# One fixed order for three engines, carried on through block 0's first layer

## The chip, the cores and the metric

The kernel runs on one core of a Trainium2 chip. A core has a matrix engine (TensorE, PE in the rows), VectorE (DVE), ScalarE (ACT), GpSimd (POOL) and a queue engine (SyncE, SP) that issues the transfers. The metric is the device time of one execution in microseconds, as the median of several runs.

## The reference

Eight heads of attention over chunks of 64 tokens make x of 4608 x 512; two layers with hidden widths of 2048 and 1024 follow.

```python
scores = (q_c @ k_c.T) / 8                       # per head, chunks of 64 tokens
attn = exp(scores - max); attn /= sum(attn) + 1e-9
x = attn @ v_c                                   # then as [4608, 512]
h = x @ w_in; y = (h * sigmoid(h)) @ w_out       # 512 -> 2048 -> 512
h = y @ w_in2                                    # 512 -> 1024
solu = h * softmax(h)
out = (layernorm(solu) * g_ln) @ w_out2          # 1024 -> 512
```

## The kernel before, in words

The tokens are worked in 9 blocks of 512, each of four tiles of 128 (block 0 has tiles 0 to 3, block 1 tiles 4 to 7, which come in the order 4, 6, 5, 7). Every fp32 operand is split into a high and a low fp16 half, and a product takes three matmuls (high by high, high by low, low by high). Blocks 0 and 1 multiply plainly; from block 2 on a form with seven products of half blocks is used.

The weights come as 64-bit words, 48 items of 512 KB: 16 of the first layer, 16 of the second, then those of the last two. SP fetches an item (`fetch`, L929, tile `wst`, four buffers, so that item i is fetched when item i - 4 has been decoded). Then it is decoded: `d1` scales on ACT (L133, into a bank of PSUM), `d2` joins bits in three DVE instructions (L140, L141, L143), and `d3` splits, the high half on ACT (L114), the low one on POOL (L118). `weights(n)` does n times d3, d1, d2.

In block 0's first layer PE works 16 groups of 12 matmuls (`h_group`, L418 to L420). Each is followed by a Silu on ACT (L422) and by `g_split`: the high half of the gate on ACT, the low half on DVE (L119). PSUM's eight banks go round in the order of the program, so a group or a d1 can need the bank whose gate low was eight allocations earlier.

Behind the groups come eight steps (`step(s)`, each followed by half of one of the four output tiles of the second layer: `x_part`, 24 matmuls, L716 to L718). The steps hold block 1's attention: q, k and v of a tile are halved (`prep_qk`, `prep_v`: ACT high, POOL low, v's low on DVE), then scores (`a_scores`: L232 to L234 on PE, the maximum L236 and the subtraction L245 on DVE, the exponential on ACT), the division (`a_norm`), a transposing transfer issued by SP (L260), and the product with v (`a_pv`, L277 to L279). `AT_S` says in which steps the scores of tiles 4, 6, 5 and 7 stand; the products stand in steps 3, 4, 6 and 7.

What sets the order: a scheduler orders the instructions by the order of the program and by priorities. The list `START` overrides it for ACT, DVE and PE up to the end of block 0's attention: each of its steps is held behind the last instruction that earlier steps put on each engine (`queue`). In the kernel before, the list ends ahead of the first layer. There the table `NW0` says how many items are decoded behind each group, and block 1's halvings of q, k and v are held behind the last step of the list alone.

Of the kernel before, what the change touches and what calls it, by code (L numbers as in the profile page):

```python
# [11 lines left out]
AF = mybir.ActivationFunctionType  # L12
# [11 lines left out]
TPB = BLK // P  # L24
NB = NT // BLK
KD = DM // P
K1 = F1 // P
# [9 lines left out]
S_X = 2.0 ** 10  # L37
# [9 lines left out]
def fused(ctx: ExitStack, tc: tile.TileContext, qkv, w1, w2, w3, w4, g_ln, out):  # L47
# [6 lines left out]
    GH = A  # L54
    FIRST = 'qqqwqvwvwvvw'
    START = ('s0 m0 s1 m1 e0 s2 s3 e1 n0 m2 m3 d1 t0 e2 p0 n1 e3 a2 n2 t1 x0 t2 n3 p1 d1 d2 x1 d3 l0 t3 l1 p2 x2 d2 '
             'd1 l2 p3 x3 d3 l3 d2 d1 d3 d2 d1 d3 d2 d1')
    AT_S = (0, 1, 3, 4)
    NW0 = [2, 0, 0, 0, 3, 0, 2, 0, 1, 0, 3, 0, 1, 0, 3, 0]
    NX = [2, 3, 2, 1, 0, 6, 0, 2]  # L60
    NW1 = [2, 1, 2, 1, 1, 1, 1, 1, 1, 1, 1, 1, 1, 1, 1, 0]
    NX1 = [1, 0, 0, 1, 0, 1, 1, 0]
# [128 lines left out]

    def prep_qk(t, eng_l=G, ahead=True):
        with ExitStack() as behind_all:
            if t // TPB == 1:
                for i in queue.values():
                    behind_all.enter_context(tc.issue_after(i))
            qk_halves(t, eng_l, ahead)

# [10 lines left out]

    def prep_v(t):  # L210
        with ExitStack() as behind_all:
            if t // TPB == 1:
                for i in queue.values():
                    behind_all.enter_context(tc.issue_after(i))
            v_halves(t)

# [184 lines left out]
            split(y[:, 0], y[:, 1], t[i].rearrange("p t k n -> p (t k) n"), 1.0, A, V)  # L401


    gt, graw = {}, {}

    def g_of(b, f):
        if (b, f) not in gt:
# [5 lines left out]
    def h_group(b, f):  # L413
        xh, xl = xt[b][:, 0], xt[b][:, 1]
        wh, wl = w1t[f][:, 0], w1t[f][:, 1]
        ps = ps1.tile([P, BLK], F32, tag="mm", name="h_ps")
        for k in range(KD):
            T.matmul(ps, wh[:, k], xh[:, k], start=k == 0, stop=False)  # L418
            T.matmul(ps, wh[:, k], xl[:, k], start=False, stop=False)
            T.matmul(ps, wl[:, k], xh[:, k], start=False, stop=k == KD - 1)  # L420
        g = one.tile([P, BLK], F32, tag=f"h{f % 2}", name="g") if b else ps
        A.activation(g, ps, AF.Silu, scale=1.0 / (S_X * S_W))  # L422
        graw[f] = g

    def g_split(b, f, eng_h=V):
        return split(*g_of(b, f), graw.pop(f), S_G, eng_h, V)

# [537 lines left out]
    def weights(n=1):  # L967
        for _ in range(n):
            d3()
            d1()  # L970
            d2()
# [12 lines left out]
    nc.sync.dma_start(out=gs, in_=g_ln)  # L984


    parts = dict(s=f_scores, m=f_max, e=f_exp, a=f_sum, n=f_norm, t=f_turn, p=f_pv, x=f_high, l=f_low)
    steps = {"d1": d1, "d2": d2, "d3": d3, "w": weights}
    queue = {}
    for x in START.split():  # L990
        with ExitStack() as behind_all:
            for i in queue.values():
                behind_all.enter_context(tc.issue_after(i))
            done = steps[x]() if x in steps else parts[x[0]](int(x[1]))
        for i in done:
            queue[i.engine] = i

    load_v(TPB)
    second = [one.tile([P, NS, P], F16, tag=f"xb{i}", name="qb") for i in range(2)]
# [4 lines left out]
    for b in range(NB):  # L1004
        m = b * TPB + TPB
        more = b + 1 < NB
        if FAST <= b:
            q_alloc(b)
        for f in range(K1):
            if b < FAST:  # L1010
                if b == 1 and f in MHF:
                    n = MHF.index(f)
                    run(m_h(b - 1, MO[n], "m1", ("m2", ("h4", "h5"), ("h6", "h7"), ("h2", "h3"))[n]))
                if b == 1 and f in MOF:
                    run(m_out(b - 1, MO[MOF.index(f)]))
                h_group(b, f)
                if b == 0:
                    weights(NW0[f])
                    if f:
                        g_split(b, f - 1, GH)  # L1020
                else:
                    y = g_split(b, f, A)
                    with tc.high_priority(offset=-50):
                        weights(NW1[f])
                    with tc.high_priority(offset=1):
                        for p in range(8):
                            if W1F[p] == f:
                                w1_sums(p)
                    if f == QF:
                        load_qk(m, ("q8",))  # L1030
                        prep_qk(m, ahead=False)
            elif f % 8 == 0:
                if f and more:
                    load_qk(m, ("w1_14", "w1_15"))
                    prep_qk(m, ahead=False)
                if b == FAST:
                    for n in range(2):
                        run(m_h(b - 1, MO[f // 4 + n], *(("m1", "m2"), ("w2_5", "w2_4"))[n % 2]))
                if f and b == FAST:
                    for n in range(2):  # L1040
                        run(m_out(b - 1, MO[n]))
                elif b > FAST:
                    run(m_fast(b - 1, 1) if f else begun, in_turn(*(m_out(b - 1, MO[n]) for n in range(2) if f)))
                run(h_fast(b, f // 4), h_fast(b, f // 4 + 1))
        if b == 0:
            g_split(b, K1 - 1, GH)
        else:
            run(m_out(b - 1, MO[TPB - 2], low=more))
        if b == FAST - 1:
            ring.load()  # L1050
        def step(s):

            if not more:
                return
            if s == 0:
                if b < FAST - 1:
                    load_qk(m)
                    prep_qk(m)
                else:
                    load_qk(after(m))  # L1060
                prep_v(m)
            if b and s == 1:
                run(m_out(b - 1, MO[TPB - 1]))
            for i in VL.get(s, ()) if b >= FAST else ():
                load_v(m + ORDER[i] if i < TPB else after(m + ORDER[-1]))
            AT_P = (3, 4, 6, 7) if b == 0 else (3, 4, 5, 6)
            if s in AT_S:
                i = AT_S.index(s)
                n = m + ORDER[i]
                a_scores(n)  # L1070
                if i < 3:
                    prep_qk(m + ORDER[i + 1], V if b == 1 else G)
                a_norm(n, eng_l=V if b else G)
            if s in AT_P:
                i = AT_P.index(s)
                a_pv(m + ORDER[i])
            if b == 0:
                with tc.high_priority(offset=-50):
                    weights(NX[s])
            if b == FAST and s in W3S:  # L1080
                w3_sums(W3S.index(s))
            if b == 1:
                weights(NX1[s])
            for n in range(4):
                if b == 1 and W2F[n] == s:
                    w2_sums(n // 2, n % 2)

        if b < FAST:
            for s in range(8):
                step(s)  # L1090
                x_part(b, s // 2, s % 2)
        else:
            begun = m_fast(b, 0, alt=not more)
            x_fast(b, step, begun)
# [54 lines left out]
```

## Time and profile before

| | |
|---|---|
| median of 3 runs | 1174.11 us (1173.61 to 1174.71) |
| the profiled execution's own time | 1173.64 us |
| its span | 1171.9 us |
| busy over the span | PE 1123.9 (96 %), DVE 917.4 (78 %), ACT 803.3 (69 %), POOL 250.4 (21 %) |
| PE's mean granted clock | 0.993 |

The profile is of one execution; times count from the start of its span, and 1.7 us of the execution lie outside it. PE's share is an average over all 9 blocks. The change lies in the first 130 us, where the weights are decoded beside the work.

### The profile page before, as it was taken

To read this page: it belongs to the slowest core of one execution; us is meant where nothing else is said; L and a number is where in the kernel's file an instruction comes from. 1 tells how busy PE (TensorE), PEld (TensorE's weight loads), DVE (VectorE), ACT (ScalarE), POOL (GpSimd) and SP (SyncE) were. 2 spreads that over 40 slices of the span, in tenths; PEclk is the share of its full clock that TensorE was granted. 3 is DMA by queue.
4 is the path that set the end of the run, shared out by engine and by line. 5 is a ranking of instruction groups with operands and counts; after the bars stand their busy time and mean duration, and the time that the engine had idled before them with its cause. 6 is when DMAs were issued, how large, how long until landed. Compare 5 with 4: busy or idle time off the path is not lost.

```text
span 1171.9 us, 23546 instructions
## 1 busy us (share of the span) xinstructions
PE 1123.9 (96%) x9036; PEld 767.0 (65%) x9036; DVE 917.4 (78%) x1639; ACT 803.3 (69%) x1460; POOL 250.4 (21%) x243
## 2 busy tenths in 40 slices
PE   7899898998999999999999999999999999999998
PEld 5344343444657865887678767876787777777853
DVE  6898998587678788889778987898689868886453
ACT  6986678675667777856775687568756875587253
POOL 3655323344101510021003100310021002100001
PEclk8999999999999999999999999999999999999999
DMA  7657488543537654786568557856776667565604
GB/s 280 217 186 209 150 234 270 166 140 113 140 113 222 180 157 132 200 228 179 150 189 235 175 157 192 230 169 160 179 235 173 162 177 223 168 163 145 207 19 117
DMA packets 205169, 209.18 MB, mean 178 GB/s; under 512 B 120192, under 2 KB 130432, under 8 KB 205056
## 3 DMA queue, kind: packets, MB, share of 16 engines
q1 hardware_dynamic: 205056, 207.68, 61.8%
q8 instruction: 70, 1.15, 0.4%
q14 instruction: 43, 0.35, 0.1%
HBM read 156.24 MB, written 24.12 MB: 154 GB/s over the span
## 4 chain that ended last, share of the span: by engine, by line
PE 64%; DVE 13%; ACT 9%; issue 6%; DMA 5%; POOL 2%; ACTq 0%; SPq 0%; POOLq 0%; DVEq 0%
PE o_ps L894 5%; PE o_ps L887 5%; PE o_ps L886 5%; PE pa L655 4%; PE pa L654 4%; PE pa L656 4%; PE pa L547 3%; PE pa L549 3%; PE pa L548 3%; PE pa L781 2%; PE pa L779 2%; PE pa L780 2%; DVE vbl L119 2%; PE pb L549 2%; PE pb L547 2%
## 5 line engine op out<-in xcount | busy, mean ns | idle before, releaser
L114 ACT ACTIVATE q<-hc 128x512 f16<-128x512 f32 x196 | 120.5, 627 | 42.8 <-DVE hc L634 15.6
L119 DVE SCALAR_TENSOR_TENSOR q<-hc,q 128x512 f16<-128x512 f32 x196 | 137.9, 719 | 10.9 <-ACT q L114 8.7
L118 POOL TENSOR_TENSOR qbl<-qk,qbh 64x512 f16<-64x512 f32 x54 | 71.2, 1319 | 264.7 <-ACT qbh L114 220.3
L654 PE MATMUL pa<-q,ring 128*128 128x256 f16 x448 | 122.1, 273 | 0.0
L656 PE MATMUL pa<-q,ring 128*128 128x256 f16 x448 | 122.1, 273 | 0.0
L655 PE MATMUL pa<-q,ring 128*128 128x256 f16 x448 | 122.1, 273 | 0.0
L886 PE MATMUL o_ps<-w4h,uT 128*128 128x512 f16 x288 | 109.1, 379 | 0.3 <-DVE e L837 0.3
L887 PE MATMUL o_ps<-w4l,uT 128*128 128x512 f16 x288 | 109.2, 379 | 0.0
L850 POOL TENSOR_TENSOR c<-c,mhalf 128x2 f32<-128x2 f32 (+1 forms) x22 | 14.1, 639 | 387.3 <-DVE c L849 385.1
L548 PEld LDWEIGHTS <-ring 128*128 128x128 f16 x784 | 77.0, 98 | 16.7 <-issue 6.1
L547 PEld LDWEIGHTS <-ring 128*128 128x128 f16 x784 | 77.0, 98 | 11.3 <-DMA ring<-w1s 0.7
L655 PEld LDWEIGHTS <-ring 128*128 128x128 f16 x784 | 76.7, 98 | 11.1
L654 PEld LDWEIGHTS <-ring 128*128 128x128 f16 x784 | 76.7, 98 | 11.1
L549 PEld LDWEIGHTS <-ring 128*128 128x128 f16 x784 | 77.0, 98 | 9.2
L656 PEld LDWEIGHTS <-ring 128*128 128x128 f16 x784 | 76.7, 98 | 8.8
L894 PE MATMUL o_ps<-w4h,uT 128*128 128x512 f16 x288 | 70.2, 379 | 0.0
L547 PE MATMUL pa<-xb,ring 128*128 128x256 f16 x224 | 61.0, 273 | 3.5 <-DVE hc L605 3.1
L547 PE MATMUL pa<-x,ring 128*128 128x256 f16 x224 | 61.0, 273 | 2.0 <-ACT hc L565 2.0
L549 PE MATMUL pa<-x,ring 128*128 128x256 f16 x224 | 61.2, 273 | 0.0
L549 PE MATMUL pb<-x,ring 128*128 128x256 f16 x224 | 61.1, 273 | 0.0
L548 PE MATMUL pb<-x,ring 128*128 128x256 f16 x224 | 61.1, 273 | 0.0
L654 PE MATMUL pb<-q,ring 128*128 128x256 f16 x224 | 61.1, 273 | 0.0
(282 smaller groups left out, 3483.7 us busy)
## 6 DMA issues: line engine op xcount, KB each, us to landing
ring<-w1s SPq DMA_DIRECT2D x196, 256.0 KB, 3.3
ring<-w2s SPq DMA_DIRECT2D x196, 256.0 KB, 3.7
wst<-w SPq DMA_DIRECT2D x48, 512.0 KB, 4.2
qk<-qkv SPq DMA_DIRECT2D x29, 512.0 KB, 3.9
vs<-qkv SPq DMA_DIRECT2D x36, 256.0 KB, 2.9
out<-o SPq DMA_DIRECT2D x36, 256.0 KB, 2.3
w1s<-ws SPq DMA_DIRECT2D x32, 128.0 KB, 2.0
w2s<-ws SPq DMA_DIRECT2D x16, 256.0 KB, 2.0
```

Source lines behind the costliest of these rows:

```text
L114: ready[0] = A.activation(dst_h, src, AF.Copy, scale=scale).ins
L118: return G.tensor_tensor(out=dst_l, in0=src, in1=dst_h, op=ALU.subtract).ins
L119: return V.scalar_tensor_tensor(out=dst_l, in0=src, scalar=scale, in1=dst_h, op0=ALU.mult, op1=ALU.subtract).ins
L547: T.matmul(ps[:, c], wh, x[:, 0, k], start=first, stop=False, skip_group_check=True)
L548: T.matmul(ps[:, c], wh, x[:, 1, k], start=False, stop=False, skip_group_check=True)
L549: T.matmul(ps[:, c], wl, x[:, 0, k], start=False, stop=k == 1, skip_group_check=True)
L654: T.matmul(ps[:, c], wh, g[:, 0], start=first, stop=False, skip_group_check=True)
L655: T.matmul(ps[:, c], wh, g[:, 1], start=False, stop=False, skip_group_check=True)
L656: T.matmul(ps[:, c], wl, g[:, 0], start=False, stop=q == 1 and f == 3, skip_group_check=True)
L886: T.matmul(ps, uh[:, k], w4h[:, k, :], start=k == 0, stop=False)
L887: T.matmul(ps, uh[:, k], w4l[:, k, :], start=False, stop=False)
L894: T.matmul(ps, ul[:, k], w4h[:, k, :], start=False, stop=k == K2 - 1)
```

## The change

The list goes on. `START` loses its last four steps, the loop over it becomes the function `in_order`, and block 0's first layer calls it for each group f with `d1 d3 d2 h{f} g{f}`: decode, group and gate are now held behind one another on each engine, where the scheduler placed them before. Behind the layer come two more d1 and one set of weights, outside the list. Of block 1's halvings only those of tile 4 are held, q and k behind gate 14's split and v behind gate 15's; the other tiles' halvings are free. In block 0 the scores of tiles 4 and 6 stand one step later each, those of the last two where they were.

```diff
     START = (...
-             'd1 l2 p3 x3 d3 l3 d2 d1 d3 d2 d1 d3 d2 d1')
+             'd1 l2 p3 x3 d3 l3 d2 d1 d3 d2')
-    NW0 = [2, 0, 0, 0, 3, 0, 2, 0, 1, 0, 3, 0, 1, 0, 3, 0]
...
     def prep_qk(t, eng_l=G, ahead=True):
         with ExitStack() as behind_all:
-            if t // TPB == 1:
-                for i in queue.values():
+            if t == TPB:
+                for i in gates[14]:
                     behind_all.enter_context(tc.issue_after(i))
...
     def prep_v(t):
         with ExitStack() as behind_all:
-            if t // TPB == 1:
-                for i in queue.values():
+            if t == TPB:
+                for i in gates[15]:
                     behind_all.enter_context(tc.issue_after(i))
...
     def g_split(b, f, eng_h=V):
-        return split(*g_of(b, f), graw.pop(f), S_G, eng_h, V)
+        low = split(*g_of(b, f), graw.pop(f), S_G, eng_h, V)
+        if b == 0:
+            gates.append((ready[0], low))
+        return low
...
+    def in_order(xs):
+        for x in xs.split():
+            with ExitStack() as behind_all:
+                for i in queue.values():
+                    behind_all.enter_context(tc.issue_after(i))
+                done = steps[x]() if x in steps else parts[x[0]](int(x[1:]))
+            for i in done:
+                queue[i.engine] = i
+
+    in_order(START)
...
-                h_group(b, f)
                 if b == 0:
-                    weights(NW0[f])
-                    if f:
-                        g_split(b, f - 1, GH)
+                    in_order(f"d1 d3 d2 h{f} g{f}" if f else "h0 g0")
                 else:
+                    h_group(b, f)
                     y = g_split(b, f, A)
...
         if b == 0:
-            g_split(b, K1 - 1, GH)
+            d1()
+            weights()
+            d1()
...
-            if s in AT_S:
-                i = AT_S.index(s)
+            at_s = AT_S if b else (1, 2, 3, 4)
+            if s in at_s:
+                i = at_s.index(s)
```

How the rows move. On DVE, in the middle of the first layer, before (`g<-h_ps,g` is a gate's low half, `wp` and `wy` are a decode's tiles):

```order
L119 SCALAR_TENSOR_TENSOR g<-h_ps,g 128x512
L143 SCALAR_TENSOR_TENSOR wy<-wst,wp 128x512
L119 SCALAR_TENSOR_TENSOR g<-h_ps,g 128x512
L140 TENSOR_SCALAR wp<-wp 128x512 x2
L141 SCALAR_TENSOR_TENSOR wp<-wst,wp 128x512 x2
L143 SCALAR_TENSOR_TENSOR wy<-wst,wp 128x512 x2
```

and in the changed kernel, where every slot reads like this one:

```order
L118 SCALAR_TENSOR_TENSOR g<-h_ps,g 128x512
L139 TENSOR_SCALAR wp<-wp 128x512
L140 SCALAR_TENSOR_TENSOR wp<-wst,wp 128x512
L142 SCALAR_TENSOR_TENSOR wy<-wst,wp 128x512
L118 SCALAR_TENSOR_TENSOR g<-h_ps,g 128x512
```

Before, decodes of two items and gates are mixed; now each slot is one decode of three instructions in a row and one gate.

On ACT at the end of the layer, before (`wp<-wst` is d1, `w2t<-wy` is d3, `h_ps<-h_ps` the Silu, `qbh` and `kb` belong to tile 4):

```order
L133 ACTIVATE wp<-wst 128x512 x2
L114 ACTIVATE g<-h_ps 128x512
L422 ACTIVATE h_ps<-h_ps 128x512
L114 ACTIVATE w2t<-wy 128x512
L114 ACTIVATE g<-h_ps 128x512
L133 ACTIVATE wp<-wst 128x512
L422 ACTIVATE h_ps<-h_ps 128x512
L114 ACTIVATE w2t<-wy 128x512
L114 ACTIVATE g<-h_ps 128x512
L114 ACTIVATE qbh<-qk 64x8x64
L133 ACTIVATE wp<-wst 128x512
L114 ACTIVATE qbh<-qk 64x8x64
```

and in the changed kernel, up to tile 4's k:

```order
L132 ACTIVATE wp<-wst 128x512
L113 ACTIVATE w2t<-wy 128x512
L132 ACTIVATE wp<-wst 128x512 x2
L113 ACTIVATE qbh<-qk 64x8x64
L132 ACTIVATE wp<-wst 128x512
L421 ACTIVATE h_ps<-h_ps 128x512
L113 ACTIVATE w2t<-wy 128x512
L113 ACTIVATE g<-h_ps 128x512
L113 ACTIVATE qbh<-qk 64x8x64
L113 ACTIVATE kb<-qk 128x512
L113 ACTIVATE vbh<-vs 64x8x64 x2
```

Three d1 (items 19 to 21, the first two in one row) and half of tile 4's q now stand ahead of the last Silu, the rest of tile 4's q and its k behind the last gate.

On DVE around tile 4's first reduce (`am<-s_ps`, L236 before, L235 now), before:

```order
L119 SCALAR_TENSOR_TENSOR g<-h_ps,g 128x512
L143 SCALAR_TENSOR_TENSOR wy<-wst,wp 128x512
L119 SCALAR_TENSOR_TENSOR g<-h_ps,g 128x512
L140 TENSOR_SCALAR wp<-wp 128x512
L236 TENSOR_REDUCE am<-s_ps 128x8
L141 SCALAR_TENSOR_TENSOR wp<-wst,wp 128x512
L119 SCALAR_TENSOR_TENSOR g<-h_ps,g 128x512
L245 TENSOR_TENSOR ae<-s_ps,am 128x512
```

and in the changed kernel:

```order
L118 SCALAR_TENSOR_TENSOR g<-h_ps,g 128x512
L142 SCALAR_TENSOR_TENSOR wy<-wst,wp 128x512
L140 SCALAR_TENSOR_TENSOR wp<-wst,wp 128x512
L118 SCALAR_TENSOR_TENSOR vbl<-vs,vbh 64x8x64 x2
L142 SCALAR_TENSOR_TENSOR wy<-wst,wp 128x512
L139 TENSOR_SCALAR wp<-wp 128x512 x2
L140 SCALAR_TENSOR_TENSOR wp<-wst,wp 128x512 x2
L142 SCALAR_TENSOR_TENSOR wy<-wst,wp 128x512 x2
L139 TENSOR_SCALAR wp<-wp 128x512
L140 SCALAR_TENSOR_TENSOR wp<-wst,wp 128x512
L142 SCALAR_TENSOR_TENSOR wy<-wst,wp 128x512
L139 TENSOR_SCALAR wp<-wp 128x512
```

Before, the reduce stands ahead of the last gate's low half; now it stands behind it, behind v's two lows and behind four more decodes (24 instead of 20). On PE one thing moves: before, the scores of tile 4 stand ahead of the second layer's first half and those of tile 6 ahead of its second; now each stands one half later. On SP the load of tile 5's q and k, which stood among the first loads, now stands behind the fetch of item 23, since its buffer is freed by tile 4's k.

## Rows read from the trace of the kernel before

**Rows 1.** Windows: each engine's busy us (x instructions), PE's clock, DMA share, GB/s.
```profile
core 0: us, PE busy (x) PEld busy (x) DVE busy (x) ACT busy (x) POOL busy (x), PEclk, DMA share, GB/s
24.00:70.00 46.00, 42.10 (x205) 18.96 (x205) 40.57 (x67) 38.30 (x69) 25.87 (x23) 1.00 0.63 211
70.00:100.00 30.00, 25.00 (x185) 12.63 (x181) 27.55 (x48) 23.96 (x54) 21.65 (x19) 0.94 0.66 191
100.00:130.00 30.00, 25.34 (x198) 12.62 (x196) 27.02 (x44) 18.69 (x45) 11.40 (x9) 1.00 0.61 188
130.00:195.00 65.00, 57.66 (x281) 27.34 (x280) 61.66 (x111) 51.58 (x90) 23.66 (x23) 1.00 0.75 221
```

**Rows 2.** Timeline of PE, 37 to 131 us: start, us, instruction [idle before <-releaser].
```profile
37.76 0.38 PE L418 MATMUL h_ps<-x,w 128*128 128x512 f16 x1 [0.63 <-DVE g L119]
...
46.30 0.38 PE L418 MATMUL h_ps<-x,w 128*128 128x512 f16 x1 [3.20 <-DVE g L119]
...
73.38 0.38 PE L716 MATMUL x_ps<-g,w2t 128*128 128x512 f16 x1 [2.91 <-DVE g L119]
...
92.58 0.20 PE L277 MATMUL x_ps<-pT,vbh 128*128 128x64 f16 x1 [2.10 <-DMA pT<-ae]
...
128.57 0.38 PE L418 MATMUL h_ps<-x,w 128*128 128x512 f16 x1 [1.26 <-ACT x L114]
```

**Rows 3.** Timeline of DVE, one decode and the next one's start.
```profile
23.93 0.69 DVE L140 TENSOR_SCALAR wp<-wp 128x512 int32<-128x512 int32 x1
24.66 0.69 DVE L141 SCALAR_TENSOR_TENSOR wp<-wst,wp 128x512 int32<-128x512 int32 x1
25.39 0.69 DVE L143 SCALAR_TENSOR_TENSOR wy<-wst,wp 128x512 int32<-128x512 int32 x1
25.99 0.69 DVE L140 TENSOR_SCALAR wp<-wp 128x512 int32<-128x512 int32 x1
```

**Rows 4.** Timeline of DVE around tile 4's first reduce.
```profile
74.15 0.69 DVE L119 SCALAR_TENSOR_TENSOR g<-h_ps,g 128x512 f16<-128x512 f32 x1 [0.23 <-ACT g L114]
74.75 0.69 DVE L140 TENSOR_SCALAR wp<-wp 128x512 int32<-128x512 int32 x1
75.35 0.68 DVE L236 TENSOR_REDUCE am<-s_ps 128x8 f32<-128x512 f32 x1
```

**Rows 5.** Timeline of ACT at the end of block 0's first layer.
```profile
71.47 0.62 ACT L133 ACTIVATE wp<-wst 128x512 f32<-128x512 f32 x1 [1.53 <-DMA wst<-w]
...
74.58 0.55 ACT L422 ACTIVATE h_ps<-h_ps 128x512 f32<-128x512 f32 x1
...
77.22 0.63 ACT L114 ACTIVATE qbh<-qk 64x512 f16<-64x512 f32 x1
...
77.87 0.63 ACT L114 ACTIVATE kb<-qk 128x512 f16<-128x512 f32 x1
...
78.52 1.28 ACT L246 ACT_TABLE_LOAD   x1
```

**Rows 6.** The tile wst on SP's queue, issues of 0:130 and of 66:71.
```profile
DMA to landing us min/median/max: 3.2/4.6/9.9
...
DMA to landing us min/median/max: 4.6/4.7/4.9
```

**Rows 7.** Timeline of POOL, lows of tile 4 and of its numerators.
```profile
76.87 2.38 POOL L118 TENSOR_TENSOR qbl<-qk,qbh 64x512 f16<-64x512 f32 x2
...
86.58 1.15 POOL L258 TENSOR_TENSOR ae<-ae 128x512 f16<-128x512 f32 x1
```

**Rows 8.** Timeline of PE, 155 to 200 us (block 1).
```profile
161.19 0.38 PE L418 MATMUL h_ps<-x,w 128*128 128x512 f16 x1 [1.66 <-ACT g L422]
...
179.33 0.27 PE L447 MATMUL wq<-w,ident 128*128 128x256 f16 x1 [2.86 <-DVE e L837]
```

**Rows 9.** Windows of 2 us each, columns as in rows 1.
```profile
74.00:76.00 2.00, 2.00 (x11) 0.91 (x10) 1.85 (x4) 2.00 (x5) 1.12 (x2) 1.00 0.59 190
...
94.00:96.00 2.00, 2.00 (x6) 0.76 (x5) 1.53 (x4) 1.18 (x2) 1.79 (x3) 0.50 0.74 197
...
96.00:98.00 2.00, 2.00 (x11) 0.83 (x9) 1.90 (x4) 1.19 (x3) 1.64 (x2) 0.95 0.97 278
```

More of the change, by code (lines that the diff above doesn't have):

```diff
@@ L401, in x_sums @@
             split(y[:, 0], y[:, 1], t[i].rearrange("p t k n -> p (t k) n"), 1.0, A, V)
-    gt, graw = {}, {}
+    gt, graw, gates = {}, {}, []
     def g_of(b, f):
@@ L419, in h_group @@
             T.matmul(ps, wh[:, k], xl[:, k], start=False, stop=False)
-            T.matmul(ps, wl[:, k], xh[:, k], start=False, stop=k == KD - 1)
+            i = T.matmul(ps, wl[:, k], xh[:, k], start=False, stop=k == KD - 1).ins
         g = one.tile([P, BLK], F32, tag=f"h{f % 2}", name="g") if b else ps
-        A.activation(g, ps, AF.Silu, scale=1.0 / (S_X * S_W))
+        j = A.activation(g, ps, AF.Silu, scale=1.0 / (S_X * S_W)).ins
         graw[f] = g
+        return [i, j]
     def g_split(b, f, eng_h=V):
-        return split(*g_of(b, f), graw.pop(f), S_G, eng_h, V)
+        low = split(*g_of(b, f), graw.pop(f), S_G, eng_h, V)
+        if b == 0:
+            gates.append((ready[0], low))
+        return low
     def flat(a, keep):
@@ L984, in fused @@
     nc.sync.dma_start(out=gs, in_=g_ln)
-    parts = dict(s=f_scores, m=f_max, e=f_exp, a=f_sum, n=f_norm, t=f_turn, p=f_pv, x=f_high, l=f_low)
+    parts = dict(s=f_scores, m=f_max, e=f_exp, a=f_sum, n=f_norm, t=f_turn, p=f_pv, x=f_high, l=f_low,
+                 h=lambda f: h_group(0, f), g=lambda f: [g_split(0, f, GH), ready[0]])
     steps = {"d1": d1, "d2": d2, "d3": d3, "w": weights}
     queue = {}
[L990 to L996, printed above, removed]
+    def in_order(xs):
[7 more added lines that the diff above has]
+    in_order(START)
     load_v(TPB)
```

## The prediction

> **What bounds the kernel now.** I read the windows by stage first, then TensorE's (PE's) waits in order of time, then the rows of the engines it waits for. The stages show two engines close to full: from 24 to 195 us VectorE (DVE) is busy 88 to 95 % of each stretch, and PE 83 to 92 % [rows 1]. The reader is to see that DVE leaves 10.9 us unused between 24 and 130 us, and 3.3 us between 130 and 195, and that PE's stops here are nearly all releases by DVE, or by ScalarE (ACT) waiting on DVE [rows 2]. So every microsecond PE gains before 130 us counts only if DVE, too, gets through its share of decoding and splitting sooner.
>
> Names: h0 to h15 are the groups of block 0's first layer, d2(i) the three DVE instructions that decode weight item i, "gate low" the DVE instruction that ends a gate's split, s4 the scores of token tile 4 and pv4 their product with v, X0a to X3b the eight halves of the second layer.
>
> **Sizes from rows.** Between the starts 37.76 (h5) and 46.30 (h7) lie two groups and a stop of 3.20, so 24 matmuls take 5.34 with the tail of the last, a group some 2.59 us, an X half 5.2 [rows 2]. From X0a's start at 73.38 to the stop before pv4 (92.58 less 2.10) lie three halves and two scores, 17.1 us: 0.8 per scores. A decode whose three instructions follow each other directly takes 0.73 + 0.73 + 0.60 = 2.06 [rows 3]; a gate low costs 0.60, as does a decode instruction that does not use its forerunner's result [rows 4].
>
> **The h groups.** In the new order each slot has one d1, one d3, the Silu and the gate's high half on ACT (about 0.5 to 0.6 each by the starts in [rows 5], 2.1 together) and d2 plus a gate low on DVE: 2.06 + 0.60 = 2.66 us against PE's 2.59. DVE sets the pace, PE hardly falls behind. The stops of 0.63 and 3.20 go: they stood behind gate lows that waited while all of block 1's first halvings passed ACT, and three tiles' halvings are now later. h15 ends at 37.76 - 0.63 + 11 x 2.59 = 65.6 instead of 69.6. On DVE: d2(2) and d2(3) end at 23.93 + 2 x 2.06 = 28.05; the first gate follows the table load of 1.28, which ends no earlier than 27.8, Silu and high half: 28.9. Then 0.60 + 2.06 and 13 more slots of 2.66: d2(17) ends at about 66.2. DVE loses by chaining (0.26 a slot, some 3.5 us) about what it idled for before in 24 to 70 (46 less 40.57 = 5.4 us [rows 1]).
>
> **The end of the layer.** Here the new order has costs. ACT holds d1(19), d1(20), d1(21) ahead of the last Silu. Item 21 is fetched into the buffer that d2(17) frees, at 66.2, and a fetch takes 4.7 us at this place (3.2 to 9.9 over the stage) [rows 6]: landed 71.0, d1(21) done 71.6, Silu 15 done 72.1, one d3, gate high 73.2, gate low 73.8. The same wait stands in the trace of before: d1 at 71.47 after 1.53 idle, last Silu 74.58 [rows 5]. Against that the gates end some 3 us sooner. Only behind them come tile 4's second q half and k on ACT (0.65 each), and two lows on POOL of 1.2 each in a row [rows 7]: k is ready at 73.2 + 0.65 + 2.4 = 76.2. X0a runs meanwhile (67.0, when the gate low that frees its bank is through, to 72.2; before it stopped 2.91 for this and started at 73.38). PE then stops some 4 us, s4 runs 76.2 to 77.0, X0b to 82.2, s6 to 83.0.
>
> **Tile 4's softmax.** On DVE its first reduce stands behind 24 whole decodes, in before behind 20, at 75.35 [rows 4]. Behind the last gate low (73.8) it has 15 instructions ahead of it, 9.1 us, and the last of them needs d1(24): fetched only after tile 5's q and k (behind the low at 76.2 on SP's queue) and d3(23). I put 1.5 us of waits there: reduce at 84.5, 9.1 late. X1a takes the bank that the subtraction behind this reduce frees, so it starts at 86.5 instead of 83.0, a second stop. From reduce to pv4 it took 92.58 - 75.35 = 17.2; ACT's queue ahead of the exponential is about as long as before, and the POOL low (86.58 in before [rows 7]) has about one more instruction ahead: 17.2 to 18.5. pv4 at 102.5, 9.9 later than before; PE stops some 9.5 us ahead of it.
>
> **What is given back.** Behind pv4 stand five halves, one scores and four pv, 5 x 5.2 + 5 x 0.8 = 30 us. Before it took 36.0 to block 1's first matmul [rows 2]; the other 6 were stops and a slow clock. With more decodes done (by the order 26 instead of 23 when tile 4's softmax ends), most of those stops go: block 1 starts at 102.5 + 30 + about 0.7 = 133, 4.5 late. At that place 37 decodes are done instead of 35: 2 x 1.8 (interleaved) to 2 x 2.06 = 3.6 to 4.1 us of DVE's work. Block 1 needs just that: DVE has 3.3 us of slack from 130 to 195, and PE stops there for 1.66 and 2.86 [rows 8], 4.5 us which a DVE that is ahead shortens. By the fourth tile's SoLU both orders have done equally many decodes. Net 4.5 - 3.6 to 4.1 = +0.4 to +0.9. The count of DVE's idle time agrees roughly: up to the last gate low even, then 1.5 at the reduce and some 2 where tile 5's subtraction waits for tile 4's transpose, less 1 to 2 of the stops after 100 us: +1 to +3. I take **+1.2**. The profiled execution took 1173.64, which is 0.47 under the median of the runs, so the forecast on the median is 1174.11 + 1.2 = **1175.3 us**. I call that no change: 0.2 % or 2.35 us is about what a measurement of this kernel can tell.
>
> **TensorE's clock.** Behind the stop of 2.10 ahead of pv4 the granted clock stood at 0.50 from 94 to 96, the level of 1.2 GHz, and was back at 0.95 in 96 to 98; behind the longer stop of 2.91 before X0a it was 1.00 from 74 to 76 [rows 2, 9]. Two us at half speed cost 1 us. The new stops of 4, 3.5 and 9.5 us may bring the half level three times; the first two would be swallowed by pv4's wait, the third is paid in before as well. The Trainium skill (TensorE: Matmul & The Clock Gate, section "Why this matters for your kernels") warns of just such idle gaps between bursts of matmuls and speaks against this change; by it, one more fall outside a wait would make the sum about 1 us longer, by the rows it stays as it is.
>
> **The rivals.** (1) Faster. The waits for fetches at the end of the layer don't occur: from the gate low 14 at 66.8, DVE has 22 instructions up to the reduce, 13.2 us, so it stands at 80.1 if nothing is waited for. pv4 then comes at 98, block 1 starts at 128.5 as before, but with two decodes in hand: 1173.6 - 3.8 = about **1170**. It decides itself by when item 21 lands: at 3.2 us it is 69.4, and 1.5 of the 4.4 us are won. For it speaks that PE's stops of 0.63, 3.20 and 2.91 do go; against it that 4.7 is the time of fetches at this place. (2) Slower. The lead in decodes buys nothing, since the stops in block 1 are released by a gate's high half and by the SoLU's exponentials, which hang on PE's own results rather than on decoding [rows 8]. Then the late start stays: 1174.1 + 4.5 = 1178.6, and 1179.6 with a clock fall. It decides at block 1's start: anything later than 131 us that is still there at 195. For it: pv4 is 9.9 late with 30 us of PE work behind it. Against: DVE is 95 % busy in block 1. (3) The change spoils PE's pace in the h groups: POOL's low takes 1.2 per slot and has room, ACT has 0.5 us of slack per slot; a slot of 2.9 instead of 2.66 would cost 3 us, 1178. I count it with (2).
>
> **How the numbers follow.** Even ledger, within 2.35 us: 0.37. Rival 1 or a milder form of it: 0.31. Rivals 2 and 3: 0.32. The even case's own range is 1172 to 1176.5; the range that holds 8 in 10 reaches from rival 1 to rival 2 with the clock, 1169.5 to 1180.
>
> **What would show it.** Right: no PE stop over 1 us between 37 and 65 us; h15's end near 65.7; the last Silu behind a d1 that waits for a fetch; s4 near 76 and a long stop before pv4, at about 102; block 1's first matmul near 133, and its stops shorter than in [rows 8]. Wrong: pv4 under 98 (then rival 1), or DVE idle over 4 us between 75 and 102 and block 1's stops unchanged (rival 2).

## The result and the profile after

The change makes the kernel slower: 1184.37 us (1182.11 to 1185.67, 6 runs) against 1173.84 us (1173.22 to 1174.71, 6 runs) before, a ratio of 1.0086 with a 95% interval of 1.0073 to 1.0099. The forecast was 1175.3 us, in a range up to 1180: wrong, on the side of rival 2. The profiled execution took 1182.84 us (span 1181.1).

The windows by stage, columns as in [rows 1]:

```profile
24.00:70.00 46.00, 44.86 (x202) 19.96 (x202) 43.08 (x67) 39.09 (x68) 22.58 (x20) 0.97 0.63 201
70.00:100.00 30.00, 19.28 (x135) 9.36 (x133) 25.47 (x41) 22.56 (x50) 22.25 (x19) 0.86 0.59 188
100.00:130.00 30.00, 26.33 (x196) 13.44 (x197) 28.07 (x45) 20.02 (x46) 14.08 (x12) 0.86 0.74 195
130.00:195.00 65.00, 58.05 (x300) 27.67 (x301) 58.23 (x107) 49.28 (x86) 23.31 (x22) 1.00 0.75 215
```

PE has gained 2.8 us of work up to 70 us, and loses 5.7 us in the next 30. The timeline of PE, with the idle time ahead in brackets:

```profile
67.81 0.38 PE L719 MATMUL x_ps<-g,w2t 128*128 128x512 f16 x1 [1.14 <-ACT w2t L113]
...
75.34 0.19 PE L231 MATMUL s_ps<-kb,qbh 128*128 128x64 f16 x1 [2.19 <-ACT kb L113]
...
77.59 0.19 PE L232 MATMUL s_ps<-kb,qbh 128*128 128x64 f16 x1 [2.06 <-POOL kb L117]
...
88.39 0.59 PE L719 MATMUL x_ps<-g,w2t 128*128 128x512 f16 x1 [2.43 <-DVE ae L244]
...
103.32 0.23 PE L276 MATMUL x_ps<-pT,vbh 128*128 128x64 f16 x1 [7.36 <-DVE am L235]
...
136.50 0.38 PE L417 MATMUL h_ps<-x,w 128*128 128x512 f16 x1 [0.55 <-ACT x L113]
...
182.30 0.38 PE L417 MATMUL h_ps<-x,w 128*128 128x512 f16 x1 [3.33 <-ACT g L421]
...
187.73 0.27 PE L450 MATMUL wq<-w,ident 128*128 128x256 f16 x1 [2.25 <-DVE e L840]
```

From 24 to 67 us PE has no stop (the two in [rows 2] are gone). Then come the forecast ones: at tile 4's scores, at X1a (88.39) and ahead of pv4. For the last of these the row names a reduce that was long over; pv4's transposed tile landed at 103.28, just ahead of it. Block 1 starts at 136.50 instead of 128.57, 7.9 us late; the span ends 9.2 us late.

ACT at the end of the layer:

```profile
71.84 0.63 ACT L132 ACTIVATE wp<-wst 128x512 f32<-128x512 f32 x1 [1.60 <-DMA wst<-w]
72.41 0.55 ACT L421 ACTIVATE h_ps<-h_ps 128x512 f32<-128x512 f32 x1
```

and DVE's last gate low and tile 4's first reduce:

```profile
74.02 0.69 DVE L118 SCALAR_TENSOR_TENSOR g<-h_ps,g 128x512 f16<-128x512 f32 x1 [2.52 <-ACT g L113]
...
75.84 2.25 DVE L118 SCALAR_TENSOR_TENSOR vbl<-vs,vbh 64x512 f16<-64x512 f32 x2
...
85.76 0.70 DVE L139 TENSOR_SCALAR wp<-wp 128x512 int32<-128x512 int32 x1 [1.23 <-ACT wp L132]
86.37 0.68 DVE L235 TENSOR_REDUCE am<-s_ps 128x8 f32<-128x512 f32 x1
```

This is the walk of the prediction: d1(21) behind its fetch (issued at 67.22, landed after 4.59 us), last Silu (72.41; 72.1 forecast), gate low (74.02; 73.8), then the reduce, 1.9 us later than forecast.

### The profile page after: what moved, and what is told of

Read it like the earlier page. It is cut to its first block, busy times and chain, and to the rows that moved or that the text cites. A ratio compares the mean times of both kernels' runs of the same rounds, so it can differ in the third digit from the quotient of the medians.

```text
span 1181.1 us, 23544 instructions
## 1 busy us (share of the span) xinstructions
PE 1128.4 (96%) x9036; PEld 768.3 (65%) x9036; DVE 920.7 (78%) x1639; ACT 805.8 (68%) x1460; POOL 251.1 (21%) x243
## 3 DMA queue, kind: packets, MB, share of 16 engines
q8 instruction: 70, 1.15, 0.4%
## 4 chain that ended last, share of the span: by engine, by line
PE 67%; DVE 14%; ACT 7%; issue 5%; DMA 4%; POOL 2%; SPq 0%; ACTq 0%; DVEq 0%; POOLq 0%
PE o_ps L897 5%; PE o_ps L889 5%; PE o_ps L890 5%; PE pa L659 4%; PE pa L657 4%; PE pa L658 4%; PE pa L550 4%; PE pa L552 4%; PE pa L551 3%; PE pa L784 2%; PE pa L782 2%; PE pa L783 2%; DVE vbl L118 2%; PE pb L550 2%; PE pb L552 2%
## 5 line engine op out<-in xcount | busy, mean ns | idle before, releaser
L550 PE MATMUL pa<-x,ring 128*128 128x256 f16 x224 | 61.3, 274 | 2.1 <-ACT hc L568 2.1
L552 PE MATMUL pa<-x,ring 128*128 128x256 f16 x224 | 61.4, 274 | 0.0
L551 PE MATMUL pa<-x,ring 128*128 128x256 f16 x224 | 61.3, 274 | 0.0
L552 PE MATMUL pb<-x,ring 128*128 128x256 f16 x224 | 61.1, 273 | 0.0
```

The costliest lines, as they stand in the source:

```text
L550: T.matmul(ps[:, c], wh, x[:, 0, k], start=first, stop=False, skip_group_check=True)
L551: T.matmul(ps[:, c], wh, x[:, 1, k], start=False, stop=False, skip_group_check=True)
L552: T.matmul(ps[:, c], wl, x[:, 0, k], start=False, stop=k == 1, skip_group_check=True)
```

## The experiments

Each ratio is against runs of the kernel before on the same chip. Those runs had medians of 1171.6 to 1172.3 us, so differences are taken chip by chip. "Late" means against the first trace of the kernel before. Letters name theories as they were held when each text was written; each text says what its letter expects.

### The parts of the change

**The list alone:** block 1's halvings held and the scores placed as before.

```diff
-            if t == TPB:
-                for i in gates[14]:      (prep_v: gates[15])
+            if t // TPB == 1:
+                for i in first:          # = list(queue.values()) behind in_order(START)
...
-            at_s = AT_S if b else (1, 2, 3, 4)
+            at_s = AT_S
```

> The list goes on through the first layer; block 1's halvings are held as before (behind the list's first part) and the scores stand in the steps of before. Theory A (the time is lost because tile 4's attention comes late: k halved behind the last gates, its first reduce behind 24 decodes; the lead in decodes that stands against it buys nothing in block 1): both causes are gone, the reduce stands behind 19 decodes, pv4 near 92, total 1168 to 1175. Theory B (the list itself costs: decodes chained on DVE at 2.06 each, ACT and DVE forced into one order): 1181 to 1186, as the changed kernel. Theory C (the loss comes from another order in block 1, made by the scheduler): total anywhere, but pv4 early and the lag arising after 136 us.

1184.08 us, 1.0100 [1.0083, 1.0117]. The reduce is on time (75.25), yet block 1 starts at 141.78, 13.2 us late: PE stops for decodes (3.60 and 2.35, both released by DVE's `wy`), 3.34 ahead of pv4 and for v's halves in later products (1.84, 1.20, 1.22 and 2.26). The total is that of theory B: the list has a cost of its own.

**The list with the old holds** (the new places of the scores kept; the first hunk alone):

> The list goes on, the halvings are held as before, the scores stand one step later as in the changed kernel. The reduce stands behind 24 decodes, as in the changed kernel, but k is ready early. Theory A with the steps as the main part: reduce near 82 to 84, pv4 near 99, total 1178 to 1182. Theory A with the hold as the main part: total 1172 to 1176. Theory B: 1181 to 1186.

1180.67 us, 1.0074 [1.0057, 1.0090]; block 1 at 136.93, and the reduce later than forecast, at 88.35.

**The list and the gates' holds, scores at their old places** (the second hunk alone):

> The changed kernel with the scores in the steps of before (tile 4 ahead of the second layer's first half). k is still halved behind gate 14, so PE waits for s4 until about 76 us in one stop of some 10 us, but the reduce stands behind 20 decodes instead of 24 (near 78). Theory A with the steps as the main part: pv4 near 95, total 1170 to 1176. Theory A with the hold as the main part: 1182 to 1188. Theory B: 1181 to 1186.

1180.91 us, 1.0082 [1.0067, 1.0097]. Tile 4's scores wait 8.38 us, block 1 starts at 136.6. With the list on, either of the other two edits takes some 3 us off its 12.5, with intervals that overlap its own; with both, which is the change, it is 10.5.

**No list:** the changed kernel with the old `START`, `NW0` and loop of the layer; the gates' holds and the new places stay.

> The other way round: order of decodes, groups and gates as before (table of counts, no list in the first layer), but the holds behind gates 14 and 15 and the later steps of the changed kernel. The reduce stands behind 23 decodes. Theory A: 1180 to 1188. Theory B: 1172 to 1176.

1176.32 us, 1.0043 [1.0028, 1.0058], at the upper end of theory B; block 1 starts 6.0 late.

**The later places alone**, in the kernel before:

```diff
-            if s in AT_S:
-                i = AT_S.index(s)
+            at_s = AT_S if b else (1, 2, 3, 4)
+            if s in at_s:
+                i = at_s.index(s)
```

> The kernel before with the scores one step later for tiles 4 and 6, nothing else: no list, halvings as before. The reduce stands behind 23 decodes as in the run without a list that also had the gates' holds (ratio 1.0043, block 1 6.0 us late). Theory G with the reduce's place as the cause: block 1 starts 4 to 6 us late, ratio 1.003 to 1.005. If the holds behind the gates were the cause: 0.999 to 1.002.

1176.68 us, 1.0037 [1.0024, 1.0050], as theory G had it with the reduce's place as the cause. The reduce stands behind 23 decodes instead of 20 and runs 6.4 us late, pv4 8.2 late. PE's stop ahead of pv4 and block 1's first matmul in its trace:

```profile
100.74 0.24 PE L277 MATMUL x_ps<-pT,vbh 128*128 128x64 f16 x1 [10.96 <-DMA pT<-ae]
...
133.47 0.38 PE L418 MATMUL h_ps<-x,w 128*128 128x512 f16 x1 [0.51 <-ACT x L114]
```

and block 1's first Silus in it, on ACT:

```profile
143.89 0.60 ACT L422 ACTIVATE g<-h_ps 128x512 f32<-128x512 f32 x1
145.47 0.58 ACT L422 ACTIVATE g<-h_ps 128x512 f32<-128x512 f32 x1
148.98 0.58 ACT L422 ACTIVATE g<-h_ps 128x512 f32<-128x512 f32 x1
152.29 0.58 ACT L422 ACTIVATE g<-h_ps 128x512 f32<-128x512 f32 x1
156.78 0.58 ACT L422 ACTIVATE g<-h_ps 128x512 f32<-128x512 f32 x1
```

In the kernel before these five start at 139.00, 140.59, 144.10, 147.41 and 151.87: 4.88 to 4.91 late, one like the other. At the sixteenth Silu it is still 5.1, and the measured time is 4.5 us longer. The same in the kernel without the list: 6.02 to 6.04 late from block 1's first Silu to its fifteenth. Both have 35 decodes done at block 1's start, as before, so there is no lead; what they show is that lateness alone passes through block 1's first layer nearly unchanged.

**The kernel before, once more** (a second trace):

> The kernel before once more, unchanged, for a second trace of it: where the granted clock falls, and whether the times at which tile 4's reduce, pv4 and block 1 start agree with the first trace to 0.5 us. Expected: agreement, with the half clock at another place in the first 30 us.

1172.32 us. Block 1 starts at 127.98; first Silu, reduce and pv4 come 0.6 to 1.0 us sooner than in the first trace, so the agreement to 0.5 us was missed. Late times well over 1 us are more than these two traces differ by.

### The lead in decodes

**More early decodes in the kernel before:**

```diff
-    NX = [2, 3, 2, 1, 0, 6, 0, 2]
+    NX = [3, 4, 3, 2, 0, 6, 0, 2]
```

> The kernel before with four more decodes in block 0's first four steps (3 4 3 2 instead of 2 3 2 1): the third and fourth reduce stand behind five to six more items, no list, no other hold. Theory G: block 1 starts 6 to 9 us later though nothing else is changed, and it doesn't come back: ratio 1.005 to 1.008. Theory H: 0.999 to 1.002.

1190.22 us, 1.0162 [1.0143, 1.0180]. Its reduce is on time (74.16) and pv4 only 2.7 late, but the next product of v waits:

```profile
111.58 0.23 PE L277 MATMUL x_ps<-pT,vbh 128*128 128x64 f16 x1 [9.58 <-ACT vbh L114]
...
146.01 0.38 PE L418 MATMUL h_ps<-x,w 128*128 128x512 f16 x1
```

Here 41 decodes are done at block 1's start, a lead of six, and block 1 starts 17.4 us late. At its sixteenth Silu it is still 16.7. Block 1 is later than either text had it. A table of five traces, counted from decodes' and matmuls' rows (a decode counts when its last instruction has ended); by the prediction a lead of one decode gives back 1.8 to 2.06 us:

```
kernel               lead  late at block 1's start  span against 1171.9  given back  priced at
later places alone     0            4.9                    +3.8              1.1        0
no list                0            6.0                    +4.4              1.6        0
the change             2            7.9                    +9.2             -1.3        3.6 to 4.1
list alone             2           13.2                   +11.1              2.1        3.6 to 4.1
more early decodes     6           17.4                   +15.0              2.4       10.8 to 12.4
```

Traces of one kernel differ, too (the second one of before has a span of 1170.5). By the end of the span, what has come back is 1.1 and 1.6 us without any lead and 2.4 with one of six.

**Fewer early decodes** in the changed kernel:

```diff
-    NX = [2, 3, 2, 1, 0, 6, 0, 2]
-    NW1 = [2, 1, 2, 1, 1, ...]
+    NX = [0, 1, 3, 3, 2, 3, 2, 0]
+    NW1 = [3, 2, 2, 1, 1, ...]
```

> The changed kernel with the decodes of block 0's eight steps moved back (0 1 3 3 2 3 2 0 instead of 2 3 2 1 0 6 0 2, and two of them into block 1): tile 4's reduce stands behind 21 decodes instead of 24, tile 6's behind 23 instead of 26, and at block 1's first matmul some two fewer are done. Theory G (what is late is the attention, since DVE does decodes ahead of it that are needed only later; the decodes are not time won, since in block 1 PE is full until 160 us and decoding ends at 142 us anyway): reduce near 81, pv4 near 97, block 1's start 131 to 133 instead of 136.5, ratio 1.003 to 1.006. Theory H (the fixed order within the first layer costs, whatever DVE does behind it): block 1's start and the ratio as in the changed kernel, 1.008 to 1.010.

1183.24 us, 1.0095 [1.0080, 1.0110], theory H's range; block 1 at 134.76. Only 34 decodes are done there, and PE, 6.2 us late, is 10.1 late at the eighth group of block 1's first layer. Decoding is not over at 142 us, as the text has it: in the kernel before the last decode's last instruction starts at 181.56.

**The same on the list alone:**

> The list with the halvings held and the scores placed as in the kernel before, and the same later decodes as in the run above: reduces behind 19, 21, 26 and 27 decodes (before: 20, 23, 28, 29). Theory G: pv4 near 94, block 1's start 129 to 131, ratio 0.999 to 1.003. Theory H: 1.007 to 1.012.

1181.04 us, 1.0079 [1.0064, 1.0094]; block 1 starts at 132.24, 9.5 sooner than in the list alone, but the ratio only falls from 1.0100 to 1.0079: new stops at 153.51 (1.18, released by POOL's low half of a decoded item) and at 168.09.

### The end of the layer

**The decodes behind the layer put in the list:**

```diff
-            d1()
-            weights()
-            d1()
+            in_order("d1 d3 d1 d2 d1")
```

> The changed kernel with the decode steps behind the layer put into the list, behind the last gate, so that the last Silu no longer stands behind d1 of items 19 to 21 and their fetches. Theory D: last Silu near 66.5 instead of 72.4, k ready and s4 some 4 to 5 us sooner, PE's stop there gone; but later decodes, so the reduce behind its 24 decodes gains little: block 1 starts 1 to 4 us sooner, ratio 1.005 to 1.008. Theory F (the fetches of items 19 to 21 behind the Silu are the main cost of the list): ratio 1.000 to 1.003.

1180.93 us, 1.0072 [1.0057, 1.0087], theory D's range. Tile 4's scores come 2.2 us sooner (73.1), pv4 at 102.89 hardly, block 1 at 135.75.

**Tile 4's holds at gates 9 and 10** (`gates[14]` to `gates[9]`, `gates[15]` to `gates[10]`):

> The changed kernel with tile 4's q, k held behind gate 9 and v behind gate 10 instead of 14 and 15. k is ready at about 58. Theory D: the stops of 2.2 and 2.1 at s4 go, but the first subtraction behind 24 decodes still holds X1a and pv4: stop at X1a longer, block 1 starts 0 to 2 us sooner, ratio 1.006 to 1.009. If the hold itself were the main cost: ratio 1.002 or less.

1182.15 us, 1.0092 [1.0074, 1.0110]. X0a now follows at 70.97, but the reduce stays at 86.82: it waits in DVE's order of decodes, not for its scores.

**The end held and fewer early decodes**, both edits:

> The changed kernel with the last decode steps held behind the last gate and the later decodes of the runs above. k comes some 5 us sooner and the reduce stands behind 22 decodes. Theory G: reduce near 79, pv4 near 95, block 1's start 129 to 131, ratio 1.000 to 1.004. Theory H: 1.006 to 1.010.

1178.07 us, 1.0052 [1.0037, 1.0067]. pv4 comes at 90.49, before its old time, and block 1 at 130.73; still the run ends 5 to 6 us late, between the two theories.

**The end held, `NX = [0, 2, 3, 3, 1, 5, 1, 1]`, tile 8's halvings held as in the run behind the next heading:**

> Three repairs together: the last decode steps of the list behind the last gate, the steps' decodes moved back but so that block 1's first matmul finds as many done as before (22, 24, 27, 28 decodes ahead of the four reduces, 35 at the last x), tile 8 held. If the lag comes from these three (theories G and C): block 1's start 130 to 132, ratio 1.000 to 1.004, and it may beat the kernel before. If the list as such costs (theory H): 1.005 or more.

1177.05 us, 1.0038 [1.0024, 1.0053], the best with the list. Block 1's start is repaired (129.25, 0.7 late), and then new stops open in block 1:

```profile
149.43 0.59 PE L738 MATMUL h_ps<-w3q,x 128*128 128x512 f16 x2 [0.43 <-ACT w3q L113]
151.19 0.81 PE L738 MATMUL h_ps<-w3q,x 128*128 128x512 f16 x3 [1.17 <-POOL w3q L117]
...
165.47 0.38 PE L417 MATMUL h_ps<-x,w 128*128 128x512 f16 x1 [1.70 <-ACT g L421]
```

`w3q` are decoded items of the third layer: decodes that were moved back are now late. The ratio lies in the first of the two ranges, but the run does not beat the kernel before.

### TensorE's clock

**Matmuls put into the new stops** of the changed kernel: 9 ahead of tile 4's scores, 26 ahead of pv4, into the bank that the real products then overwrite, so nothing is left out.

```diff
+        if t == TPB:                     # a_scores: 9; a_pv: 26, with g_of(0, 15)
+            for _ in range(9):
+                T.matmul(ps.rearrange("p s i -> p (s i)"), w1t[0][:, 0, 0], g_of(0, 14)[0], start=True, stop=True)
```

> The changed kernel with 9 matmuls that do no needed work ahead of tile 4's scores and 26 ahead of its pv4, each 128x512 into the bank that the real ones then start afresh, so that PE is busy for 1.9 and 5.6 us of the stops of 4.3 and 7.4. Theory D (block 1 starts late by the sum of PE's stops and of what the half clock behind them adds, about half each, and nothing of it comes back because PE was full in block 1 before, too): the clock stays near 1.00 from 90 to 110, block 1 starts 3 to 5 us earlier than in the changed kernel (132 to 133.5), total 3 to 5 us shorter, ratio 1.004 to 1.006. Theory E (only the waits for DVE count, the clock is hidden by them): ratio 1.008 to 1.010, as the changed kernel.

1188.76 us, 1.0144 [1.0128, 1.0161]. pv4 has no stop and a full clock, but later products wait 3.54 and 1.40 us for v's halves, and block 1 starts at 141.84. Neither range holds. The added work also shifted the order of decodes, so this run is not clean.

**The same in the kernel before**, 8 matmuls ahead of pv4:

> The kernel before with 8 such matmuls ahead of pv4, where PE stops for 2.1 us and the half level follows. Theory D: X1b at full speed, 1.2 to 1.6 us gained, ratio 0.9985 to 0.9990. Theory E: ratio 0.9995 to 1.0005.

1175.12 us, 1.0024 [1.0015, 1.0034]. Two windows of it and its waits on PE:

```profile
92.00:94.00 2.00, 2.00 (x29) 1.17 (x26) 2.00 (x5) 1.06 (x3) 2.00 (x3) 1.00 0.83 299
94.00:96.00 2.00, 2.00 (x11) 0.94 (x10) 1.90 (x4) 0.98 (x2) 2.00 (x3) 1.00 0.66 180
```

```profile
100.92 0.20 PE L280 MATMUL x_ps<-pT,vbh 128*128 128x64 f16 x1 [2.43 <-ACT vbh L114]
...
102.56 0.20 PE L282 MATMUL x_ps<-pT,vbl 128*128 128x64 f16 x1 [1.41 <-DVE vbl L119]
...
128.61 0.38 PE L421 MATMUL h_ps<-x,w 128*128 128x512 f16 x1 [1.26 <-ACT x L114]
```

The clock is 1.00 where it was 0.50 [rows 9], PE gets ahead and waits for v's halves instead; block 1 starts at 128.61, as before. Neither range holds, and where the 0.24 % arise behind block 1's start isn't shown.

### The stop at 182 us in block 1

Behind block 1's start the Silus of the changed kernel look as if something came back: 7.9 us late at the first, 3.7 at the fifth. At the eighth it is 9.0. That is ACT's order: PE's matmuls stay 7.9 late up to the seventh group, are 6.1 late at the eighth (167.30) and 9.0 at the tenth (182.30), behind the eighth Silu. The store of the weight sums (`w1s<-ws`) on SP's queue:

```profile
166.99 7.70 SPq L470 DMA_DIRECT2D w1s<-w  x14
...
176.86 0.90 SPq L476 DMA_DIRECT2D w1s<-ws  x2
```

and on ACT the half that waits for it, with tile 8's q on both sides, ahead of the Silu:

```profile
178.09 0.61 ACT L113 ACTIVATE qbh<-qk 64x512 f16<-64x512 f32 x1
180.56 0.42 ACT L113 ACTIVATE ws<-y 128x256 f16<-128x256 f32 x1 [1.85 <-DMA w1s<-ws]
181.00 0.63 ACT L113 ACTIVATE qbh<-qk 64x512 f16<-64x512 f32 x1
181.65 0.60 ACT L421 ACTIVATE g<-h_ps 128x512 f32<-128x512 f32 x1
```

**Tile 8's halvings held behind block 1's tenth Silu:**

```diff
-                        load_qk(m, ("q8",))
-                        prep_qk(m, ahead=False)
+                        with tc.issue_after(silu[9]):
+                            load_qk(m, ("q8",))
+                            prep_qk(m, ahead=False)
```

> The changed kernel, with the halving of tile 8's q and k (block 2's first tile) held behind the tenth Silu of block 1, where it stood in the kernel before; in the changed kernel it stands ahead of the eighth, in a place where the lag against before grew from 3.7 to 9.0 us. Theory C (block 1 did give back what the lead in decodes is worth, and the other order of ACT and SP in block 1 took it again): the lag stays near 4 to 6 us from there on, total 3 to 4 us shorter than the changed kernel, ratio 1.005 to 1.006. Theory G (what is late at block 1's start stays): the lag is 7 to 8 us again behind the next waits, ratio 1.008 to 1.009.

1182.16 us, 1.0080 [1.0065, 1.0095], theory G's range. ACT's half waits longer (2.35), and PE's stop stays (2.52): the halvings were only in its shadow.

**The copies `w1s<-w` held behind the last transposing transfer as well**, so that the stores go first. Tile 8's loads and halvings are held behind the tenth Silu and behind that transfer:

```diff
-                    nc.sync.dma_start_transpose(out=uT[h], in_=u[:, h])
+                    last[0] = nc.sync.dma_start_transpose(out=uT[h], in_=u[:, h]).ins
```

> The changed kernel, with the copies of the first layer's weights held behind the last transposing transfer issued so far, so that the stores of the weight sums no longer stand behind some 14 of them on SP, and with tile 8's loads and halvings held behind the tenth Silu of block 1. Theory I: of the 8 us late at block 1's start, 4 are given back by Silu 20 (a lead of two decodes does work), and are lost again at the stop of 3.3 at 182, where ScalarE waits for a store of weight sums with tile 8's q ahead of the Silu. Then this kernel reaches Silu 23 no more than 5 to 6 us late instead of 9, and ends some 3 us sooner than the changed kernel, 1178 to 1180 us. Theory J: that stop is only where the next wait shows; another takes its place (the exponentials, VectorE), Silu 23 is 8 to 10 us late and the time is 1181 to 1183 us.

1184.90 us (1181.15 to 1188.73), 1.0096 [1.0081, 1.0111], above both ranges. **The same edit in the kernel before:**

> The kernel before, with the same hold on the copies of the weights alone. It prices that edit by itself. Theories I and J both expect no change beyond 2 us, since in the kernel before the stores of the weight sums stand right behind the copies and no half of the weight sums waits over 0.4 us ahead of Silu 23: 1170 to 1174 us. If it gains 3 us or more, the gain of the other kernel is not told apart from what this edit gives any kernel.

1175.76 us, 1.0031 [1.0020, 1.0043]: by itself the edit costs 0.3 %, which neither theory expected. In the changed kernel with it the stop at 182 is gone, and PE is 9.4 to 9.6 late there after 10.9 at block 1's start. But time is not won: halvings of tile 8 and stores now come together later, and the first scores of block 2 wait 3.27 us for k.

That run of the changed kernel showed something else by chance. Up to block 1 its program is that of the changed kernel, but in the profiled execution one fetch came later:

```profile
74.44 0.62 ACT L132 ACTIVATE wp<-wst 128x512 f32<-128x512 f32 x1 [3.03 <-DMA wst<-w]
```

The fetch was issued at 68.37 instead of 67.22, since the layer already ran 1.15 us late, and took 6.05 us to land instead of 4.59. So that d1 starts 2.60 us later than at 71.84 above. Tile 4's scores come 2.60 later (77.94), its reduce 2.59 (88.96), pv4 3.19 (106.51), block 1's first matmul 3.0 (139.51), its fifth Silu 3.0. Lateness from the end of the layer passes on at least one for one, as far as this pair of traces shows.

## Why the prediction was wrong

**The step that failed is "What is given back".** It set 4.5 us late at block 1's start against 3.6 to 4.1 from a lead of two decodes. The lead was there, 37 decodes to 35, but by the end of the span nothing of the 7.9 us had come back; without a lead, lateness of 4.9 and 6.0 us passed through block 1's first layer. The reason was in the profile. From block 1's start on PE has nothing to wait for, as the window of the kernel before shows:

```profile
129.00:160.00 31.00, 30.18 (x147) 14.37 (x147) 30.43 (x47) 20.97 (x38) 10.51 (x10) 1.00 0.56 166
```

DVE is as full as PE, and I read that as a shortage which a lead relieves; but PE loses only 0.8 us in these 31, so no more than that can be won in them. A lead can only shorten stops that its work releases. One such stop there was, the 1.66 of [rows 8] at the eighth group. Its row names a Silu (L422), not a gate's high half as rival 2 said, and on ACT that Silu stands behind decode work that waited for DVE:

```profile
158.14 0.72 ACT L114 ACTIVATE w4h<-wy,gs 128x512 f16<-128x512 f32 x1 [1.80 <-DVE wy L143]
...
159.99 0.66 ACT L133 ACTIVATE wy<-wst 128x512 f32<-128x512 f32 x1 [0.34 <-DVE w4l L119]
160.56 0.58 ACT L422 ACTIVATE g<-h_ps 128x512 f32<-128x512 f32 x1
```

In the change this stop is gone and PE's lateness falls there from 7.9 to 6.1 us. It falls by 1.8, too, in the list alone and with a lead of six, by 0.9 to 1.9 in every run with a lead, and not at all in the two late runs without one. That is what the lead bought, and six decodes bought no more than two. The other stops of that stage went another way. A new one of 3.33 us opened at 182.30, the 2.86 of [rows 8], released by DVE's product in SoLU, became 2.25, and one of 2.09 went:

```profile
193.54 0.38 PE L418 MATMUL h_ps<-x,w 128*128 128x512 f16 x1 [2.09 <-DVE y L462]
```

(The second trace of the kernel before lacks this one as well.) So at its first output matmul, 202.55 instead of 196.46, the changed kernel is 6.1 late. The other 3 us up to the span's 9.2 come later, 1.2 of them at 244 to 248, where the granted clock stood at 0.78 and 0.50 behind a stop of 1.45. Rival 2 had the outcome, with too small a lateness and a reason that holds for one of its two stops.

**Block 1's start was mis-sized, 7.9 late instead of 4.5.** 0.8 of this is pv4 (103.3 for 102.5; the reduce 86.4 for 84.5, with v's two lows at 2.25 us ahead of it where 0.60 an instruction was counted). The other 2.5 lie behind pv4: 33.2 us for 30.7. At two of the windows there the clock stood at its half level, 1.2 GHz:

```profile
104.00:106.00 2.00, 2.00 (x19) 1.17 (x17) 1.86 (x3) 1.21 (x2) 0.86 (x1) 0.50 1.00 381
106.00:108.00 2.00, 2.00 (x7) 0.62 (x6) 1.45 (x4) 1.27 (x3) 0.00 (x0) 0.50 1.65 292
```

PE has only 0.34 and 0.55 us of stops between pv4 and block 1, so these 2.5 us are slow work and no wait: from pv4's start to the start of the last matmul of the half behind it took 8.2 us, against 5.7 at a clock of 1.00 in the kernel before with 8 matmuls filled in. The kernel before itself takes 7.3 there. "TensorE's clock" said that this fall is paid in before as well, but the sum of 30 us behind pv4 counts every half at full speed and so drops it. Whether a full clock would win these us is not shown: in the kernel before it moved block 1's start by nothing, since v's halves came next. The Trainium skill (TensorE: Matmul & The Clock Gate, section "Why this matters for your kernels") warns of idle gaps; the trace agrees that the clock falls in them (1.00 in 96 to 98, within the stop of 7.36, and 0.50 from 100 to 108), and the runs that filled them were slower, by 0.24 % in the clean one.

**"The h groups" and "The end of the layer" were right** within about 1 us: no stop from 24 to 67, d1(21) behind its fetch, the Silu at 72.4, k last on POOL, its low ending at 77.55 (1.50 us where 1.2 was put). The second half of the scores waited for it till 77.59 (76.2 forecast). X1a stopped (88.39 for 86.5), pv4 had the long stop ahead. **Rival 1** fell with the fetch: it landed at 71.82 (71.0 forecast). **Rival 3** did not occur; the slots kept PE's pace.

**Which edit costs it.** The list alone costs 1.00 %, and the other two edits without the list 0.43 %; together they cost 0.86 %. They don't add up: with the list on, later places and freer halvings are a partial repair. By itself the first part, 13.2 us at block 1's start, comes from PE waiting for decodes, pv4 and v's halves; its gate lows come at most 4 us sooner but for the first, and the last 1.5 later. What stays open: with the list on, no mixture of places, holds and decode tables got below 1.0038, and where block 1's start was repaired, 4 us and more arose inside block 1. Where decodes were moved back they are late there: in those four runs 34 are done at block 1's start instead of 35, PE's lateness grows by 3.2 to 3.9 us up to the eighth group, with stops that `w3q` releases on the way, and the last decode starts at 195.8 in the best of them instead of 181.6. So a lack of decodes costs, though a lead wins little. The best of them is 7.2 us ahead of the change at block 1's start and some 5.6 in the time; with fewer early decodes, the list alone wins 9.5 there and some 2.5 in the time. Why so much is lost again in the one and less in the other is not settled, and how much the chained decodes (2.06 instead of 1.8 us each) add was not isolated.

## What to carry to other kernels

Work done ahead is worth something only if a later stop is released by that work: before booking a lead as gain, take the stops it is to shorten and read, through the queue of the engine that ends them, whether that work holds them up. Those stops are the most it can win: here about 1.8 us, with two decodes or six. A stage with PE full behind a stop gives nothing back, so lateness at its entry is the price. When a fixed order removes stops early in a stage, look at what now stands last on each queue at its end, since here 2.6 us of lateness there were 3.0 at block 1's fifth Silu.

## What the runs showed of the hardware

- Filling PE's idle time with matmuls held the granted clock at 1.00 from 94 to 96 us where [rows 9] shows 0.50, and the kernel became 0.24 % slower, with block 1's start as before: the next wait took up what the clock gave.
- The same half of the second layer behind pv4, 24 matmuls, took 4.97 us from its first start to its last at a clock of 1.00 and 6.93 where the clock stood at 0.50 for the first part of it.
- The same fetch of 512 KB took 4.59 us to land in one execution and 6.05 in another, in programs that are alike up to there. With 1.15 us by which it was issued later, ACT's d1 behind it came 2.60 us later, and 3.0 us of difference remained 60 us on.
